# A two-layer decode kernel: queries and the first layer's gate and up with the weights as the moving operand

## The chip, the cores and the metric

The kernel runs on one core of a Trainium2 chip. The metric is device time in microseconds, the median of three runs. The profile is of one execution, and times inside it count from the start of its span.

## The reference

Two layers, each an attention block over a cache and a gated feed-forward block, for four sequences with one new token each:

```python
B, Sq, D = 4, 1, 512
Hq, Hkv, Sk, Dh = 32, 8, 8192, 128        # F = 1792, all bf16
def A(x, k_cache, v_cache, wq, wo):       # 4 query heads share one of the 8 cached heads
    q = (x @ wq) as (B, Hq, Sq, Dh)
    scores = einsum("bhqd,bhkd->bhqk", q, repeat(k_cache)) * Dh ** -0.5
    o = einsum("bhqk,bhkd->bhqd", softmax(scores), repeat(v_cache))
    return o as (B, Sq, Hq * Dh) @ wo
def B(x, w_gate, w_up, w_down):
    return (silu(x @ w_gate) * (x @ w_up)) @ w_down
x = x + A(layernorm(x)); x = x + B(layernorm(x))      # both twice, with the same weights
```

## The kernel before

The caches are 128 MB together and read in both layers; a few parts stay on the chip from one layer to the next. Everything else is small. So the program is written around one long stream of transfers, all issued by SyncE. Its order is the list `cmds`; `pump` issues the next entries as far as their place is free, and `freed(slot, a, b)`, called where an instruction that reads a place has been written, gives eighths (or halves of eighths) of a slot back. There are four slots of 4 MB and one more (`QS`), which first holds w_q, then K and V data.

The unit of attention work is a pair: two cached heads of one sequence, 16 pairs in a layer, K and V of a pair 4 MB each. For K, VectorE transposes blocks in place (`turn`, L558), TensorE computes scores with the queries as weights, laid out in `zq` with zeros around them (`scores`, L582), VectorE takes the maximum (`max_p`, `max_t`), ScalarE the exponential (`exps`, L629), VectorE transposes the result (`turn_p`, L646), and TensorE multiplies V (`values`, L718: four matmuls at a time, each in a quarter of the array's columns). The order of blocks is written out by hand with estimated due times (`drain`, `advance`, `line`). The output projection follows by groups of two heads and four sequences (`mix` L801, `rows` L836, `project` L861).

At the head of a layer, `center` subtracts the mean of x, and `qproj` multiplies by w_q: for every 128x128 block of w_q one matmul with that block as weights and four moving columns (L917, 128 of them a layer), then one scaling by `rstd` (L926), 16 small matmuls that bring the queries into the layout of the scores (L936), the placing of the first pair (`place_q`) and a copy for all others (L941). `deviation` (L903 to L907) computes `rstd`, with the logarithm of the scores' scale as a bias where queries are meant. In the second layer each eighth of w_q that has been read is freed for pieces of K.

At a layer's end `ffn` multiplies by gate and up with 128x128 weights and four moving columns (L961, 112 a layer), computes silu and the product (L975 to L982), and multiplies by w_down: in the first layer with w_down as weights (L999), in the second with hT as weights (L989). `WDS` lists which 128-row parts of w_down each transfer brings and how many rows stand side by side in a partition (the third number). The hidden index f must come in the same order out of gate and up; `base(L, fo)` says where the columns of part `fo` start and by how many elements they step, which is that third number.

Between the layers the slot that holds the first layer's weights is freed piece by piece by `ffn` and refilled with K of the second layer. A quarter of one K block stays in PSUM meanwhile (`hold`, L521 and L524); while it does (`held`), other small results go to bank 3.

Of the kernel before, what the change touches and what calls it, by code (L numbers as in the profile page):

```python
# [103 lines left out]
def bass_interleave_layers__gqa_block_cached__swiglu_ffn__decode_kernel(  # L104
# [40 lines left out]
    with ExitStack() as es:  # L145
# [14 lines left out]
        WDS = (((12, 14, 2), (10, 12, 2), (0, 2, 2), (2, 6, 4), (6, 10, 4)), ((0, 8, 2), (8, 12, 2), (12, 14, 2)))  # L160
# [26 lines left out]
        def base(L, fo):  # L187
            a, _, e = next(w for w in WDS[L] if w[0] <= fo < w[1])
            return a * P + (fo - a) // e * e * P + (fo - a) % e, e

        def wg_at(s, k, f, e):
            return columns(s * SL + k * F + f, e)

        def wu_at(s, k, f, e):
            o = k * F + f
            return columns((NSLOT + 1) * SL + o if o < RES else s * SL + O_WU + o - RES, e)
# [35 lines left out]
        head = sb("head", [P, H2], FP32)  # L232
        sel = sb("sel", [P, H2], FP32)
# [31 lines left out]
        qr = scr[:, 0:NQR].rearrange("p (c b g r) -> p c b g r", c=4, b=B, g=GP)  # L265
        made = scr[:, 0:2 * QB].bitcast(FP32)
        qT = scr[:, NQR:].rearrange("p (b h) -> p b h", b=B)
# [9 lines left out]
        def bank_bf(k):  # L277
# [6 lines left out]
        ROLE = {"step": (STEP, 0), "tot": (TOT, 128), "cmb": (LNB, 136), "out": (OUTB, 144), "mix": (LNB, 160), "ln": (LNB, 256),  # L284
                "q": (OUTB, 0)}
# [34 lines left out]
        for a in range(NA):  # L320
# [5 lines left out]
        T.op("dve", lambda e: e.memset(zq[:], 0.0), writes=["zq"])  # L326
# [15 lines left out]
             reads=["made"], writes=["own"])  # L342
        nc.scalar.preload_act_table_set("natural_log_exp_and_others")
# [3 lines left out]
        def pair_gb(u):  # L347
            return u // B, u % B

# [45 lines left out]
        cmds += [(K(1, us[2]), QS, a, b) for a, b in ((0, 1), (1, 2), (2, 4), (4, VIA))]  # L395
# [66 lines left out]
        def load_wd(w0, L, j, also=()):  # L462
            a, b, e_ = WDS[L][j]
            o = 0 if w0 is pTf else wd_from(L, a)
            T.dma("sp", w0[:, o:o + (b - a) * D].rearrange("p (m x) -> p m x", x=e_ * D),
                  B_w_down[a * P:b * P, :].rearrange("(m p e) n -> p m (e n)", p=P, e=e_), sem_w["wd"][j],
                  writes=[f"wd{j}"] + list(also))
# [95 lines left out]
        def place_q(L, u, eng="pool", q_of=qr, names=None):  # L563
            if (L, u) in placed_q:
                return
            placed_q.add((L, u))
            gp, b = pair_gb(u)
            shape = [P, 4, NA, REP]
            dst = zq[:, ZP:].rearrange("p (c a x) -> p c a x", c=4, a=NA)[:, :, :, 0:REP]
            q4 = q_of[:, :, b, gp, :].unsqueeze(2).to_broadcast(shape)  # L570
            m4_ = quad[:].unsqueeze(1).unsqueeze(3).to_broadcast(shape)
            T.op(eng, lambda e: e.tensor_tensor(dst, q4, m4_, ALU.mult),  # L572
                 reads=(names or ["qr"]) + ["quad"], writes=["zq"])

        def scores(L, u, q):
# [4 lines left out]
            for c in range(4):  # L580
                z0 = ZP + c * P - REP * q
                T.op("pe", lambda e: e.matmul(bank(bk)[:, 0:SW], lhsT=zq[:, z0:z0 + P], rhs=w[:, :, c // 2, :, c % 2],  # L582
                                              start=(q == 0 and c == 0), stop=(q == NB - 1 and c == 3)),
                     reads=names + ["zq"], writes=[f"pb{bk}"], sig=(c == 3))
# [29 lines left out]
        def exps(u):  # L614
            bk = SBK[turn_of[u]]
            i = turn_of[u]
            if summed:
# [4 lines left out]
            else:  # L622
# [4 lines left out]
            T.op("dve", lambda e: e.tensor_tensor_reduce(rsm, mine, head[:], 1.0, 0.0, ALU.mult, ALU.add, nm),  # L627
                 reads=[name, "head"], writes=["nm", "rsm"])
            T.op("act", lambda e: e.activation(pb[:], bank(bk)[:, 0:SW], ACTF.Exp, bias=nm, accum_out=rs),  # L629
                 reads=[f"pb{bk}", "nm"], writes=PB + ["rs"])  # L630
# [70 lines left out]
        def values(L, u):  # L701
# [71 lines left out]
            def combine():  # L773
# [5 lines left out]
                def scaled():  # L779
                    T.op("dve", lambda e: e.tensor_tensor(oT[:, gp * H2:(gp + 1) * H2, b], at, rl[:, turn_of[u], :], ALU.mult),  # L780
                         reads=[name, f"rl{turn_of[u]}"], writes=[OT[gp], "qT"])
# [10 lines left out]
        def mix(gs, fill):  # L792
# [4 lines left out]
            now = oT[:, gs[0] * H2:(gs[-1] + 1) * H2]  # L797
# [11 lines left out]
        groups = [[0, 1, 2, 3], [3, 0, 1, 2]]  # L809
        mixed, later = set(), []  # L810

        def close_group(L, gp, fill):
            if gp == groups[L][-1]:
                line.extend([[0.5, None, lambda: mix([gp], fill)], [0.7, None, lambda: out_proj(gp, fill)]])
                return
            if gp == 0:
                return
            gs = [0, 1] if gp == 1 else [gp]
            line.append([0.5, None, lambda: mix(gs, fill)])
# [13 lines left out]
        def rows(L, gp):  # L833
            for r in range(H2):
                h = gp * H2 + r
                T.op("pe", lambda e: e.matmul(bank(OUTB)[0:B, 0:D], lhsT=oT[:, h, :], rhs=wo_sb[:, h, :],  # L836
# [19 lines left out]
        def project(gp):  # L856
            at, name = place("out", 0, XB)
            for nt in range(KT):
                for r in range(H2):
                    h = gp * H2 + r  # L860
                    T.op("pe", lambda e: e.matmul(at[:, nt * B:(nt + 1) * B],  # L861
                                                  lhsT=wo_sb[:, h, pick2(nt)], rhs=oT[:, h, :],
# [3 lines left out]
        def out_proj(gp, fill):  # L866
            project(gp)
# [33 lines left out]
        def deviation(bias, bkey):  # L901
            at, name = (bank(SBK[1])[:, 0:B], f"pb{SBK[1]}") if held[0] else place("tot", 0, B)
            T.op("pe", lambda e: e.matmul(at, lhsT=ones, rhs=vs, start=True, stop=True),  # L903
                 reads=["vs", "onesf"], writes=[name])
            T.op("act", lambda e: e.activation(lnv, at, ACTF.Ln, scale=1.0 / D, bias=eps_sb[:]),
                 reads=[name, "eps"], writes=["lnv"])
            T.op("act", lambda e: e.activation(rstd[:], lnv, ACTF.Exp, scale=-0.5, bias=bias[:]),  # L907
                 reads=["lnv", bkey], writes=["rstd"])

        def qproj(L, u):  # L910
            at, name = place("ln", 0, Hq * B)
            for kt in range(KT):
                if kt == KT // 2:
                    deviation(lsc_sb, "lsc")
                for h in range(Hq):
                    q, last = 2 * kt + h * 2 // Hq, (h + 1) * 2 % Hq == 0
                    T.op("pe", lambda e: e.matmul(at[:, h * B:(h + 1) * B],  # L917
                                                  lhsT=wq_sb[:, kt, h * Dh:(h + 1) * Dh],
                                                  rhs=xn[:, kt * B:(kt + 1) * B],
                                                  start=(kt == 0 and h == 0), stop=(kt == KT - 1 and h == Hq - 1)),  # L920
                         reads=[WQ[q], "xn"], writes=[name], sig=last)
                    if L and last and q < NB - 2:
                        if q == NB - 3:
                            T._wait("act", T._need((), [WQ[q]]))
                        freed(QS, q, q + 1)
            T.op("dve", lambda e: e.tensor_tensor(qT, at.rearrange("p (h b) -> p b h", b=B),  # L926
                                                  rstd[:].unsqueeze(2).to_broadcast([P, B, Hq]), ALU.mult),
                 reads=[name, "rstd"], writes=["qT"] + OT)

            pick = ident.rearrange("p (c j e) -> p c j e", c=2, e=2)  # L930
            ob, oname = place("q", 0, NQR)
            ob = ob.rearrange("p (c b g r) -> p c b g r", c=4, b=B, g=GP)
            qv = qT.rearrange("p b (g h r) -> p b g h r", h=2, r=REP)
            for c in range(4):
                for a in range(NA):
                    T.op("pe", lambda e: e.matmul(ob[a * QB:(a + 1) * QB, c],  # L936
                                                  lhsT=pick[:, c // 2, :, c % 2],
                                                  rhs=qv[:, :, :, a // 2, :], start=True, stop=True),
                         reads=["qT", "ident"], writes=[oname], sig=(a == NA - 1))
            place_q(L, u, "dve", ob, [oname])  # L940
            T.op("dve", lambda e: e.tensor_copy(qr, ob), reads=[oname], writes=["qr", "made"])  # L941

        def ffn(L):
# [4 lines left out]
            fb = lambda ap: ap.rearrange("p (f b) -> p f b", b=B)  # L948
            rb = rstd[:].unsqueeze(1).to_broadcast([P, FO, B])
            rooms = {"wg0": room(s, 0, F), "wg1": room(s, F, 2 * F), "wg2": room(s, 2 * F, 3 * F), "wg3": room(s, 3 * F, O_WU), "wu0": [], "wu1": room(s, O_WU, O_WD)}  # L950
            for j, (a, b, _) in enumerate(WDS[L]):
# [3 lines left out]
            for at, wname, bk, ks in ((wg_at, "wg0", gb, (0, 1)), (wg_at, "wg1", gb, (1, 2)),  # L955
                                      (wg_at, "wg2", gb, (2, 3)), (wg_at, "wg3", gb, (3, KT)),
                                      (wu_at, "wu0", ub, (0, KT // 2)), (wu_at, "wu1", ub, (KT // 2, KT))):
                for fo in range(FO):
                    f = base(L, fo)
                    for kt in range(*ks):  # L960
                        T.op("pe", lambda e: e.matmul(bank(bk)[:, fo * B:(fo + 1) * B],  # L961
                                                      lhsT=at(s, kt, *f),
# [133 lines left out]
```

## Time and profile before

| | |
|---|---|
| median of three runs | 644.91 us (644.39 to 645.34) |
| the profiled execution | 645.21 us, of which the span 643.43 us |
| instructions | 7434, of which 3126 matmuls and 3128 weight loads |
| busy: PE, DVE, ACT, POOL | 65%, 66%, 7%, 2% of the span |
| DMA | 271.33 MB, the data queue's packets 99.0% of sixteen engines' span |
| mean granted clock of TensorE | 0.83 |

In lines of the profile, L and a number is a line of the kernel; "x" and a number counts instructions; PE is TensorE's matmuls, PEld its weight loads, DVE VectorE, ACT ScalarE, POOL GpSimd, SP SyncE. A timeline line has the start, the time, the engine, the line and the operation, and in brackets the idle time of the engine before it and what ended it. A line of the chain of waits has the start, the time and what the path ran through. The sixteen DMA engines share each transfer; a transfer counts as landed when all of them have finished their part.

### The profile page before, as it was taken

To read this page: it belongs to the slowest core of one execution; us is meant where nothing else is said; L and a number is where in the kernel's file an instruction comes from. 1 tells how busy PE (TensorE), PEld (TensorE's weight loads), DVE (VectorE), ACT (ScalarE), POOL (GpSimd) and SP (SyncE) were. 2 spreads that over 40 slices of the span, in tenths; PEclk is the share of its full clock that TensorE was granted. 3 is DMA by queue.
4 is the path that set the end of the run, shared out by engine and by line. 5 is a ranking of instruction groups with operands and counts; after the bars stand their busy time and mean duration, and the time that the engine had idled before them with its cause. 6 is when DMAs were issued, how large, how long until landed. Compare 5 with 4: busy or idle time off the path is not lost.

```text
span 643.4 us, 7434 instructions
## 1 busy us (share of the span) xinstructions
PE 416.7 (65%) x3126; PEld 180.0 (28%) x3128; DVE 421.7 (66%) x593; ACT 42.3 (7%) x118; POOL 11.6 (2%) x44
## 2 busy tenths in 40 slices
PE   0673376456765757757866977776555577557877
PEld 0421122112222322222226432332221232222324
DVE  5275467455776656776952688887765567755964
ACT  0000000000000000000010110000000000000110
POOL 0000000000000000000000000000000000000000
PEclk9995786698877889766975899999778887769877
DMA  9999999999999999999999999999999999999996
GB/s 372 442 424 416 430 444 426 431 424 429 438 436 423 428 433 439 426 426 431 440 406 380 416 431 431 436 429 425 432 435 432 427 430 438 429 428 429 440 408 257
DMA packets 15872, 271.79 MB, mean 422 GB/s; under 512 B 1624, under 2 KB 1632, under 8 KB 7264
## 3 DMA queue, kind: packets, MB, share of 16 engines
q1 hardware_dynamic: 15840, 271.33, 99.0%
q8 instruction: 24, 0.39, 0.2%
q14 instruction: 8, 0.07, 0.0%
HBM read 271.32 MB, written 0.00 MB: 422 GB/s over the span
## 4 chain that ended last, share of the span: by engine, by line
DMA 61%; DVE 19%; PE 15%; issue 3%; another core or an unknown queue 1%; SPq 0%; DVEq 0%
DMA kvf<-in_A_k_cache_dram 49%; DVE kvf L558 15%; DMA kvf<-in_A_v_cache_dram 11%; PE ps L582 9%; PE ps L718 2%; DVE pb L770 2%; DMA kvf<-in_B_w_down_dram 1%; PE ps L961 1%; PE ps L917 1%; DVE pb L766 0%; DVE pT L646 0%; DVE scr L780 0%; SPq L93 0%; PE ps L861 0%
## 5 line engine op out<-in xcount | busy, mean ns | idle before, releaser
L582 PE MATMUL ps<-kvf,zq 128*128 128x512 bf16 x1024 | 292.9, 432 | 183.5 <-DVE kvf L558 178.8
L558 DVE STREAM_TRANSPOSE kvf<-kvf 128x2048 f32<-128x2048 f32 (+1 forms) x133 | 280.5, 2132 | 128.4 <-DMA kvf<-in_A_k_cache_dram 128.0
L582 PEld LDWEIGHTS ps<-kvf,zq 128*128 128x128 bf16 x1024 | 99.1, 108 | 340.2 <-DVE kvf L558 222.6
L718 PE MATMUL ps<-kvf,pT 128*32 128x512 bf16 x960 | 67.6, 405 | 1.1 <-DVE pT L646 1.1
L629 ACT ACTIVATE pb<-ps,tiny 128x512 bf16<-128x512 f32 x32 | 22.0, 687 | 525.9 <-DVE tiny L627 505.1
L646 DVE STREAM_TRANSPOSE pT<-pb 64x512 bf16<-64x512 bf16 x60 | 41.2, 686 | 2.7 <-ACT pb L629 1.7
L770 DVE SCALAR_TENSOR_TENSOR pb<-ps,tiny,pb 128x128 f32<-128x128 f32 x104 | 36.5, 351 | 4.7 <-PE ps L718 0.8
L588 DVE TENSOR_REDUCE tiny<-ps 128x1 f32<-128x512 f32 x32 | 22.0, 687 | 20.1 <-PE ps L582 20.1
L718 PEld LDWEIGHTS ps<-kvf,pT 128*32 128x32 bf16 x960 | 21.0, 99 | 31.2 <-issue 16.0
L775 PEld LDWEIGHTS ps<-sel,pb 128*128 128x128 f32 x64 | 17.0, 273 | 16.5 <-DVE pb L770 8.3
L572 POOL TENSOR_TENSOR zq<-scr,tiny 128x64 bf16<-128x64 bf16 x30 | 9.0, 299 | 527.1 <-PE ps L582 527.1
L596 DVE TENSOR_REDUCE mrm<-ps 1x8 f32<-1x128 f32 x32 | 8.8, 275 | 13.6 <-PE ps L593 13.6
L775 PE MATMUL ps<-sel,pb 128*128 128x8 f32 x64 | 12.4, 267 | 5.8 <-DVE pb L770 5.8
L619 PEld LDWEIGHTS ps<-mrm,tiny 128*128 128x128 f32 x60 | 13.0, 223 | 9.2 <-DVE scr L780 3.2
L917 PE MATMUL ps<-xn,kvf 128*128 128x4 bf16 x256 | 7.5, 166 | 11.5 <-DMA kvf<-in_A_wq_dram 11.2
L766 DVE TENSOR_SCALAR pb<-ps,tiny 128x128 f32<-128x128 f32 x32 | 10.1, 315 | 3.0 <-PE ps L718 3.0
L619 PE MATMUL ps<-mrm,tiny 128*128 128x16 f32 x60 | 9.9, 241 | 3.1 <-ACT mrm L631 3.1
L836 PE MATMUL ps<-wo_sb,scr 128*4 128x512 bf16 x48 | 11.0, 379 | 0.5 <-DVE scr L805 0.5
L917 PEld LDWEIGHTS ps<-xn,kvf 128*128 128x128 bf16 x256 | 7.3, 105 | 11.8 <-DMA kvf<-in_A_wq_dram 11.4
L631 ACT ACTIVATE mrm<-head,tiny 128x8 f32<-128x8 f32 x32 | 9.6, 301 | 1.0
L593 PE MATMUL ps<-identf,tiny 128*1 128x128 f32 x32 | 8.7, 273 | 0.7 <-DVE tiny L588 0.7
L790 DVE TENSOR_TENSOR xT<-xT,ps 128x16 f32<-128x16 f32 x6 | 1.0, 171 | 10.4 <-PE ps L846 4.7
(87 smaller groups left out, 120.3 us busy)
## 6 DMA issues: line engine op xcount, KB each, us to landing
kvf<-in_A_k_cache_dram SPq DMA_DIRECT2D x27, 4096.0 KB, 31.2
kvf<-in_A_v_cache_dram SPq DMA_DIRECT2D x27, 4096.0 KB, 33.9
kvf<-in_A_v_cache_dram SPq DMA_DIRECT2D x3, 2048.0 KB, 25.2
kvf<-in_A_k_cache_dram SPq DMA_DIRECT2D x9, 512.0 KB, 7.9
kvf<-in_A_k_cache_dram SPq DMA_DIRECT2D x2, 2048.0 KB, 9.4
kvf<-in_A_wq_dram SPq DMA_DIRECT2D x2, 2048.0 KB, 18.1
wo_sb<-in_A_wo_dram SPq DMA_DIRECT2D x4, 1024.0 KB, 41.4
kvf<-in_B_w_gate_dram SPq DMA_DIRECT2D x2, 1792.0 KB, 23.9
```

The costliest lines, as they stand in the source:

```text
L558: T.op("dve", lambda e: e.transpose(w, w), reads=names, writes=names)
L582: T.op("pe", lambda e: e.matmul(bank(bk)[:, 0:SW], lhsT=zq[:, z0:z0 + P], rhs=w[:, :, c // 2, :, c % 2], start=(q == 0 and c == 0), stop=( ...
L588: T.op("dve", lambda e: e.tensor_reduce(mx[:], bank(bk)[:, 0:SW], AX.X, ALU.max), reads=[f"pb{bk}"], writes=["mx"])
L619: T.op("pe", lambda e: e.matmul(at, lhsT=ones, rhs=mrm[:, i * H2:(i + 2) * H2], start=True, stop=True), reads=[f"m8{i}", "rsm", "onesf"], ...
L629: T.op("act", lambda e: e.activation(pb[:], bank(bk)[:, 0:SW], ACTF.Exp, bias=nm, accum_out=rs), reads=[f"pb{bk}", "nm"], writes=PB + ["rs"])
L646: T.op("dve", lambda e: e.transpose(dst, pb[hp]), reads=["pb", "row"], writes=[name])
L718: T.op("pe", lambda e: e.matmul(bank(k)[j * QB:(j + 1) * QB, q0 * Dh:q1 * Dh], lhsT=p_t[:, t, h, :], rhs=v[:, q0:q1, t, :], start=((last o ...
L766: T.op("dve", lambda e: e.tensor_scalar(into, o, own[:, q:q + 1], None, op0=ALU.mult), reads=[f"pb{k}", "own"], writes=["row"] if last els ...
L770: T.op("dve", lambda e: e.scalar_tensor_tensor(into, o, own[:, q:q + 1], into, op0=ALU.mult, op1=ALU.add), reads=[f"pb{k}", "own", iname], ...
L775: T.op("pe", lambda e: e.matmul(at, lhsT=into, rhs=sel[:], start=True, stop=True), reads=[iname, "sel"], writes=[name])
L836: T.op("pe", lambda e: e.matmul(bank(OUTB)[0:B, 0:D], lhsT=oT[:, h, :], rhs=wo_sb[:, h, :], start=(gp == groups[L][0] and r == 0), stop=(g ...
L917: T.op("pe", lambda e: e.matmul(at[:, h * B:(h + 1) * B], lhsT=wq_sb[:, kt, h * Dh:(h + 1) * Dh], rhs=xn[:, kt * B:(kt + 1) * B], start=(k ...
```

## The change

Queries. `qproj` now takes the normalised x as weights (128 rows, four columns) and 512 columns of w_q as the moving operand, in each of the four quarters of the array's columns, so that one pass over a row block of w_q is two times four matmuls instead of 32. w_q's two halves of heads go to two PSUM banks. In the second layer the half that holds the first pair's heads comes first, and the freed eighths go out in that order. VectorE transposes each bank (`on_end`), four small copies place the first pair, and eight copies on ScalarE (`spread`) give the layout from which `place_q` takes the others. The queries are no longer scaled: `rstd` enters as the scale of the exponential, and `headr` (the mask of heads times `rstd`) in its bias.

First layer's gate and up. The same exchange: 448 columns of the weights move through each quarter, one matmul for each (one strip is cut in two where its data lie in two places), and VectorE transposes the two results.

w_down. Its rows are dealt differently, in both layers. In the first, partition p holds rows 14p to 14p+13. In the second, the rows side by side in a partition become 8, 4 and 2 for the three transfers (2 before), and the gate and up columns follow.

Also: output groups of the second layer are kept in the order of their use (`spot`), and its first three groups are mixed together; a VectorE memset of two PSUM banks comes at the start.

The diff, cut:

```diff
-        WDS = (((12, 14, 2), (10, 12, 2), (0, 2, 2), (2, 6, 4), (6, 10, 4)), ((0, 8, 2), (8, 12, 2), (12, 14, 2)))
+        WDS = (((12, 14), (10, 12), (0, 2), (2, 6), (6, 10)), ((0, 8), (8, 12), (12, 14)))
+        WDE = (8, 4, 2)
...
-        def base(L, fo):
-            a, _, e = next(w for w in WDS[L] if w[0] <= fo < w[1])
+        def base(fo):
+            j = next(j for j, w in enumerate(WDS[1]) if w[0] <= fo < w[1])
+            a, e = WDS[1][j][0], WDE[j]
             return a * P + (fo - a) // e * e * P + (fo - a) % e, e
...
+        T.op("dve", lambda e: e.memset(ps[:, SBK[1] * BANKF:(OBK[0] + 1) * BANKF], 0.0),
+             writes=[f"pb{SBK[1]}", f"pb{OBK[0]}"])
...
-        cmds += [(K(1, us[2]), QS, a, b) for a, b in ((0, 1), (1, 2), (2, 4), (4, VIA))]
+        cmds += [(K(1, us[2]), QS, a, b) for a, b in ((1, 2), (3, 4), (0, 1), (2, 3), (4, VIA))]
...
-            T.dma("sp", w0[:, o:o + (b - a) * D].rearrange("p (m x) -> p m x", x=e_ * D),
-                  B_w_down[a * P:b * P, :].rearrange("(m p e) n -> p m (e n)", p=P, e=e_), sem_w["wd"][j],
-                  writes=[f"wd{j}"] + list(also))
+            dst, src = w0[:, o:o + (b - a) * D], B_w_down.rearrange("(p f) n -> p (f n)", f=FO)[:, a * D:b * D]
+            if L:
+                dst = dst.rearrange("p (m x) -> p m x", x=WDE[j] * D)
+                src = B_w_down[a * P:b * P, :].rearrange("(m p e) n -> p m (e n)", p=P, e=WDE[j])
+            T.dma("sp", dst, src, sem_w["wd"][j], writes=[f"wd{j}"] + list(also))
...
-            T.op("dve", lambda e: e.tensor_tensor_reduce(rsm, mine, head[:], 1.0, 0.0, ALU.mult, ALU.add, nm),
-                 reads=[name, "head"], writes=["nm", "rsm"])
-            T.op("act", lambda e: e.activation(pb[:], bank(bk)[:, 0:SW], ACTF.Exp, bias=nm, accum_out=rs),
+            T.op("dve", lambda e: e.tensor_tensor_reduce(rsm, mine, headr[:, b, :], 1.0, 0.0, ALU.mult, ALU.add, nm),
+                 reads=[name, "headr"], writes=["nm", "rsm"])
+            T.op("act", lambda e: e.activation(pb[:], bank(bk)[:, 0:SW], ACTF.Exp, bias=nm, scale=rstd[:, b:b + 1],
+                                                  accum_out=rs),
...
-            gs = [0, 1] if gp == 1 else [gp]
+            gs = groups[L][:n + 1] if n == (1, 2)[L] else [gp]
...
+            def on_end(k):
+                src = bank(QK[k]).rearrange("p (x i e) -> p x e i", i=QB, e=2)
+                dst = bank(TO[k]).rearrange("p (i x e) -> p x e i", i=QB, e=2)
+                T.op("dve", lambda e: e.transpose(dst, src), reads=[f"pb{QK[k]}"], writes=[f"pb{TO[k]}"])
...
+            for n in range(NB):
+                k, kt = (first, 1 - first)[n // KT] if L else n % 2, n % KT if L else n // 2
+                q = 2 * kt + k
+                if n == NB // 2:
+                    scales = deviation(lsc_sb, "lsc", SBK[0], False)
+                    if L:
+                        on_end(first)
+                        place_first()
+                        scales()
+                for a in range(NA):
+                    f = ((2 * k + a % 2) * 2 + a // 2) * W2
+                    T.op("pe", lambda e: e.matmul(bank(QK[k])[a * QB:a * QB + B, :],
+                                                  lhsT=xn[:, kt * B:(kt + 1) * B], rhs=wq_sb[:, kt, f:f + W2],
+                                                  start=(kt == 0), stop=(kt == KT - 1)),
+                         reads=[WQ[q], "xn"], writes=[f"pb{QK[k]}"], sig=(a == NA - 1))
...
+                blk = bank(k)[:, 0:FW].rearrange("p (i f) -> p f i", f=FO)
+                T.op("dve", lambda e: e.transpose(blk, blk), reads=[f"pb{k}"], writes=[f"pb{k}"])
...
+                for kt in range(*ks):
+                    parts = [(0, *base(fo), fo) for fo in range(FO)] if L else [(a, f, w, 0) for a, f, w in strips(bk == ub, kt)]
+                    for n, (a, f, w, fo) in enumerate(parts):
+                        x = xn[:, kt * B:(kt + 1) * B]
+                        if L:
+                            to, lhs, rhs = bank(bk)[:, fo * B:(fo + 1) * B], at(s, kt, f, P, w), x
+                        else:
+                            to, lhs, rhs = bank(bk)[a * QB:a * QB + B, f - a * FW:f - a * FW + w], x, at(s, kt, f, w)
...
+                on_end(1 - pair_gb(us[0])[0] // 2)
+            spread()
```

## The prediction

> **What bounds the kernel now.** I read the page first: how full the DMA engines are.
>
> ```profile
> DMA  9999999999999999999999999999999999999996
> ...
> q1 hardware_dynamic: 15840, 271.33, 99.0%
> q8 instruction: 24, 0.39, 0.2%
> ```
>
> The sixteen DMA engines are busy in every slice but the last: from 3 us on, the kernel is one stream of 271 MB. What an engine saves counts only where the stream runs dry or after it ends. So next the chain of waits over the end, from the landing of the last values on.
>
> ```profile
> 585.97 43.37 DMA kvf<-in_A_v_cache_dram
> ...
> 635.46 0.84 PE ps L961 x28
> 636.29 0.22 PE ps L903 x2
> 636.52 2.22 PE ps L961 x84
> 638.74 0.52 PE ps L879 x8
> 639.26 1.49 PE ps L989 x47
> 640.75 0.03 issue
> 640.78 0.42 PE ps L989 x8
> ```
>
> The values land at 629.3; behind them stand 14 us in which nearly nothing overlaps, and 3.1 us of these are the second layer's 112 gate and up matmuls (L961) on PE. Then the boundary between the layers, by the timeline, and the same line at the end:
>
> ```profile
> 343.94 1.85 PE L961 MATMUL ps<-xn,kvf 128*128 128x4 bf16 x56
> ...
> 346.24 1.00 PE L961 MATMUL ps<-xn,kvf 128*128 128x4 bf16 x28 [0.45 <-DMA kvf<-in_B_w_up_dram]
> ```
> ```profile
> 636.38 2.36 PE L961 MATMUL ps<-xn,kvf 128*128 128x4 bf16 x84
> ...
> 639.17 1.99 PE L989 MATMUL ps<-kvf,pb 128*4 128x128 bf16 x56
> ```
>
> At the boundary PE itself waits for transfers (and again 0.90 us for w_down at 349.25); at the end its matmuls are the path. The last view is the end by stretches of 1 us (length; busy us of PE, PE's loads, DVE, ACT, POOL; clock, DMA share, GB/s):
>
> ```profile
> 638.00:639.00 1.00, 1.00 (x36) 0.96 (x33) 0.83 (x4) 0.00 (x0) 0.00 (x0) 0.50 0.32 123
> 639.00:640.00 1.00, 1.00 (x38) 0.74 (x32) 0.11 (x1) 0.00 (x0) 0.00 (x0) 0.50 0.13 49
> ```
>
> PE's clock is 0.50 here, and the DMA share (0.32, 0.13, from 1.02 at 634 to 636) falls in steps: the engines finish one by one. Each transfer is spread over sixteen and is complete with the slowest. The completion records of the last w_down transfer run from 635.98 to 640.73; those of the first K spread over 0.44 us. The slowest engine's lag over the fastest grew in steps of 1.2 to 1.4 us (0.38 to 1.59, 1.7 to 3.1, 2.1 to 3.39, 3.6 to 4.92), each beside a 16 KB packet of the instruction queue (1.0 to 1.1 us on one engine; 24 on the page). The slowest engine sets every landing.
>
> **Part by part: the w_q product.** Each layer's 128 matmuls that load 128x128 weights and the 16 that pick (L936) become 32 with 512 moving columns, four at a time in the array's quarters. The values matmuls (L718) have that form: four start within 10 ns, a round takes 216 ns at full clock and 427 ns at half. At the boundary (clock 0.50) eight rounds are 3.4 us, and the 128 loads at 26.7 ns were 3.4 us too: PE gains nothing there. What goes is the way to the first scores. After half the rounds (1.7 us) DVE transposes 512 columns (0.6 us, half of L521's 1.22 us for 1024) and four small copies of 0.2 to 0.3 us on two engines place the first pair, beside the second half. Scores start when that half ends, near 356.7 instead of 357.7. The other DVE transpose (0.6), headr (0.3) and eight ACT copies (2 us) come after the two transposes of L521, where qT, the placing and the copy (0.29, 0.23, 0.41 us) went ahead of them; the second pair needs them at 366. If that cover were gone, 3 us would show. This microsecond is worth nothing: the slots that those scores free are refilled by a queue that is not empty. The thinnest point is 343.6: what is issued then starts on the slowest engine at 347.3, more than 2 us after it could. In the first layer the first scores come about 0.7 us later (both transposes ahead of them), before a wait of 8 us for the next K (33.7). The scale in the exponential makes one operand of ACT (L629, 0.69 us) a column: nothing, or at most 0.1 us under the stream.
>
> **Pieces.** The order of K pieces into w_q's place changes, and one piece of 1 MB with 8 KB rows is now two with 4 KB rows. By the packet records (314 ns for 8 KB, 165 ns for 4 KB) that is 128x314/16 = 2.51 us against 256x165/16 = 2.64: **+0.13 us** on the stream.
>
> **First layer's gate and up.** 112 matmuls become 33 of up to 448 columns (0.37 us a round): gate 1.5 us against 1.7, the last half of up 0.8 against 1.0. Two transposes of 448 columns (0.55 us each) are added; the gate's lies under the 0.45 us wait for w_up and what slack the silu has, up's is on the path. hT comes 0.3 us later, and the next w_down group waits 0.9 us for its landing anyway: **0**. Without that cover 0.3 us of PE, not of the stream.
>
> **Second layer's w_down.** Not in the change's few words, but in its diff: the rows per partition go from 2, 2, 2 to 8, 4, 2, so packets of 2 KB (86 ns) become 8 and 4 KB. 1 MB and 0.5 MB take 2.51 and 1.32 us instead of 2.76 and 1.38, together 0.31 us, of which at most 0.2 us of wait is there to be had (L989 pauses twice).
>
> Its price: gate and up columns must follow the same order, and `base` now steps by 8 elements for 64 of those 112 weight loads, by 4 for 32, by 2 for 16; all 112 stepped by 2. Line L961 prices two steps. At the end 84 with step 2 take (2.36 - 0.17)/83 = 26.4 ns each. In the first layer, at the same clock, 32 of the 56 step by 4: (1.85 - 0.17)/55 = 30.6 on average, so (56x30.6 - 24x26.4)/32 = 33.8 ns: **+7 ns**. Step 8 (16 bytes) is not in this form in the trace; the nearest row is the load of 32 columns with that step, L801, beside L718's with none:
>
> ```profile
> L801 PEld LDWEIGHTS ps<-scr,identf x96: 134/156/165, 209.8 to 632.7; 128*32 128x32 bf16 x96
> ...
> L718 PEld LDWEIGHTS ps<-kvf,pT x960: 92/97/151, 45.4 to 625.5; 128*32 128x32 bf16 x192
> ```
>
> Median 156 against 97 ns (L936, 8 bytes apart: 126), and L801's rounds of four follow each other every 59 ns at either clock, with only 8 columns to move. I treat one load of 128 columns (26.7 ns when contiguous, L917) like four such loads side by side, an estimate, and take 59 ns: +32.3. Bounds: 26.4 (no cost), and 67 (step 4 spends 33.8 ns on 64 runs of two elements, step 8 has twice as many runs). Sum: 64x32.3 + 32x7 = **2.3 us** more PE on the path that ends last. Nothing covers it: up's end releases hT (L982), then L989; silu's 1.5 us run beside up and are longer covered. The two waits of L989 vanish in it (-0.2): **+2.1 us**; ends -0.2 and +2.6. The strided gr, gw, hT operands cost nothing: L596 reads with that step, 128 elements in 0.28 us.
>
> The Trainium skill (SBUF — State Buffer, Specifications (TRN2)) speaks against this part: lines are of 16 bytes, and full bandwidth needs at least two hits in each. By it step 4 would be free and step 8 pay; the trace agrees on the direction but already charges 7 ns for two hits.
>
> **Instruction packets.** 303 matmuls with their loads go (2x112 + 79), 606 of PE's 6254 instructions; 0.39 MB over 6254 is 63 bytes, so 38 KB or 2.3 of the 16 KB packets. About 4 of the 22 before the values' landing hit the slowest engine; 4/22 x 2.3 x 1.25 us = **-0.5 us**, an estimate. Which engine a packet hits isn't to be foreseen: bounds -1.2 and +1.2 us.
>
> **Others.** Eight output rows matmuls of the first group in the second layer move to 585 (24 in place of 16, 1.8 us more): PE is idle 4.6 us behind them.
>
> **Sum.** The profiled execution took 645.21 us (span 643.43 and 1.8 around it), 0.30 over the median 644.91. 645.21 + 2.1 + 0.13 - 0.5 = 646.9, so a median of **646.6**.
>
> **Rivals.** *The step is free.* Then the second layer's FFN costs as before, or 0.64 - 0.2 us if 8 is charged like 4. For it: step 4 cost only 7 ns; against it: L801. The Trainium skill (TensorE: Matmul & The Clock Gate, Weight-path perf modes) keeps the fast load for any column step up to 1,024 elements. 644.91 + 0.4 + 0.13 - 0.5 = 645.0, not slower; 0.20. *The step is free and the slowest engine loses a whole packet or two:* 644.91 - 0.2 + 0.13 - 1.2 = 643.6, or less; 0.10. *Quarters don't overlap:* the four strips run one after another, gate takes 16x0.37 = 6 us instead of 1.7, and what its passes free is issued up to 4 us later. It decides from the 2 us that the slowest engine has in hand: 646.6 + 2 to 4 = 649 to 651. Against it L718's starts; 0.06. Forecast: 0.62, within it 0.14 that the packets bring it under +0.2%. The rest, 0.02, anything else, slower.
>
> **Numbers.** A measurement tells about 0.2% (1.3 us) from none. The free step's 0.20 fall to 0.17 same, 0.02 slower, 0.01 faster. Slower: 0.48 of the forecast, 0.06, 0.02 and 0.02: 0.58. Same: 0.14 + 0.17 = 0.31. Faster: 0.10 + 0.01 = 0.11. The range runs from the free step with half a packet more gained (645.0 less 0.8) to the 67 ns load (+0.5), no packet gain (+0.5) and half a packet's loss (+0.6): 644.2 to 648.2.
>
> **What would show it.** L961 at the end: 84 matmuls in about 4 us instead of 2.36, at step 8 one in 59 ns; L989 without pauses; the chain unchanged up to there; the DMA row full across the boundary; w_q's line near 3.4 us plus the deviation; 21 or 22 packets on q8; the last values landing within 1.2 us of 629.3. Wrong if step 8 runs at 27 to 34 ns, if the DMA row shows a hole near 345 to 360, or if the values land more than 1.3 us away.

## The result, and the profile after

The changed kernel takes **647.31 us** (median of 6 runs, 646.29 to 647.91), the kernel before 644.86 (6 runs, 644.39 to 645.36): ratio **1.0035**, 95% interval 1.0022 to 1.0048. It is slower by 2.45 us; the forecast was 646.6 and slower. The profiled execution after took 647.37 us, with a span of 645.1 (before: 645.21 and 643.43).

The stream first, on the page after, as read before:

```profile
DMA  9999999999999999999999999999999999999995
...
q1 hardware_dynamic: 15472, 271.33, 98.8%
q8 instruction: 22, 0.36, 0.2%
```

It is as full as it was up to the last slice, across the boundary too; the 271.33 MB are the same, and two instruction packets fewer were fetched (22 for 24). Next, the chain of waits over the end, from the issue of the last values:

```profile
585.66 43.05 DMA kvf<-in_A_v_cache_dram
...
634.95 1.44 PE ps L1041 x28
636.38 0.43 PE ps L931 x2
636.81 4.03 PE ps L1041 x84
640.85 0.52 PE ps L907 x8
641.37 1.58 PE ps L1069 x42
```

The steps are the same as before, under new line numbers (L1041 was L961, L931 was L903, L907 was L879, L1069 was L989). The transfer of values on this chain lands at 628.72, 0.6 us earlier than before; the second layer's 112 gate and up matmuls then take 1.44 + 4.03 us where they took 0.84 + 2.22. The same stretch by the timeline of PE (start, length, line, matmuls; idle time ahead in brackets):

```profile
634.88 1.50 PE L1041 MATMUL ps<-xn,kvf 128*128 128x4 bf16 x28
...
636.67 4.17 PE L1041 MATMUL ps<-xn,kvf 128*128 128x4 bf16 x84
640.77 0.59 PE L907 MATMUL ps<-identf,xT 128*4 128x64 f32 x8
641.22 1.67 PE L1069 MATMUL ps<-kvf,pb 128*4 128x128 bf16 x56
```

1.50 - 0.84 and 4.17 - 2.36 make +2.47 us of PE on the path; L1069 has lost its two pauses (1.67 for 1.99). The 84 are 48 loads at step 8, 24 at step 4 and 12 at step 2: with 0.17 us off for the last matmul's own length, and 32 and 26 ns for steps 4 and 2 (priced below), (4.00 - 24 x 0.032 - 12 x 0.026)/47 = 62 ns for one at step 8.

The windows of 1 us (busy us of PE, PE's loads, DVE, ACT, POOL; clock, DMA share, GB/s) tell whether the transfers or PE held this stretch:

```profile
638.00:639.00 1.00, 1.00 (x25) 1.00 (x23) 0.73 (x3) 0.26 (x1) 0.00 (x0) 0.50 0.28 111
639.00:640.00 1.00, 1.00 (x25) 1.00 (x24) 0.72 (x2) 0.00 (x0) 0.00 (x0) 0.50 0.11 43
640.00:641.00 1.00, 1.00 (x26) 0.98 (x26) 0.12 (x1) 0.00 (x0) 0.00 (x0) 0.50 0.08 23
```

PE is full and starts 25 matmuls in a microsecond. The kernel before, on the same line and at the same granted clock of 0.50, started 44:

```profile
637.00:638.00 1.00, 1.00 (x44) 1.00 (x41) 0.62 (x3) 0.40 (x2) 0.00 (x0) 0.50 0.63 229
```

The load port was full then too, so what has changed is the time of one load. The transfers run out beside it.

The boundary between the layers, by the timeline of PE:

```profile
344.21 1.66 PE L1041 MATMUL ps<-kvf,xn 128*4 128x448 bf16 x16
346.34 0.91 PE L1041 MATMUL ps<-kvf,xn 128*4 128x448 bf16 x9 [0.47 <-DMA kvf<-in_B_w_up_dram]
...
349.49 0.59 PE L1079 MATMUL ps<-pb,kvf 128*128 128x4 bf16 x16 [0.35 <-DMA kvf<-in_B_w_down_dram]
...
352.72 1.88 PE L996 MATMUL ps<-kvf,xn 128*4 128x512 bf16 x16 [0.27 <-DVE xn L919]
354.53 0.59 PE L931 MATMUL ps<-pb,tiny 128*128 128x4 f32 x2
355.05 1.88 PE L996 MATMUL ps<-kvf,xn 128*4 128x512 bf16 x16
356.86 1.37 PE L607 MATMUL ps<-kvf,zq 128*128 128x512 bf16 x3
```

The same two places before:

```profile
349.25 0.58 PE L999 MATMUL ps<-pb,kvf 128*128 128x4 bf16 x16 [0.90 <-DMA kvf<-in_B_w_down_dram]
...
357.71 0.61 PE L582 MATMUL ps<-kvf,zq 128*128 128x512 bf16 x1 [0.35 <-DVE zq L572]
```

The quarters overlap (16 matmuls of 512 columns in 1.88 us are 0.47 us for each four), the first scores start at 356.86, 0.85 us earlier than before, and the wait for w_down has shrunk from 0.90 to 0.35 us: most of what up's transpose adds came out of that wait.

### The profile page after: what moved, and what is told of

It reads as the page before. It is cut to its first block, busy times and chain, and to the rows that moved or that the text cites. A ratio compares the mean times of both kernels' runs of the same rounds, so it can differ in the third digit from the quotient of the medians.

```text
span 645.1 us, 6824 instructions
## 1 busy us (share of the span) xinstructions
PE 414.8 (64%) x2807; PEld 172.3 (27%) x2809; DVE 426.3 (66%) x599; ACT 50.2 (8%) x138; POOL 11.9 (2%) x44
## 3 DMA queue, kind: packets, MB, share of 16 engines
q1 hardware_dynamic: 15472, 271.33, 98.8%
## 4 chain that ended last, share of the span: by engine, by line
DMA 60%; DVE 20%; PE 15%; issue 4%; ACT 0%; SPq 0%; POOL 0%; ACTq 0%; DVEq 0%; POOLq 0%
DMA kvf<-in_A_k_cache_dram 45%; DVE kvf L581 15%; DMA kvf<-in_A_v_cache_dram 11%; PE ps L607 8%; DMA kvf<-in_A_wq_dram 3%; PE ps L745 2%; DVE pb L797 2%; PE ps L1041 1%; DMA kvf<-in_B_w_down_dram 1%; PE ps L996 1%; DVE pT L673 1%; DVE pb L793 1%; DVE ps L547 0%; DVE scr L807 0%; PE ps L889 0%
## 5 line engine op out<-in xcount | busy, mean ns | idle before, releaser
L745 PE MATMUL ps<-kvf,pT 128*32 128x512 bf16 x960 | 65.8, 396 | 1.5 <-DVE pT L673 1.5
L655 ACT ACTIVATE pb<-ps,tiny 128x512 bf16<-128x512 f32 x32 | 24.9, 777 | 507.7 <-DVE tiny L653 489.2
L996 PE MATMUL ps<-kvf,xn 128*4 128x512 bf16 x64 | 7.5, 621 | 11.1 <-DMA kvf<-in_A_wq_dram 10.8
L807 DVE TENSOR_TENSOR scr<-ps,rl 128x8 bf16<-128x8 f32 x32 | 5.7, 177 | 3.2 <-PE ps L802 2.2
L745 PE MATMUL ps<-kvf 128*32 128x512 bf16 (+2 forms) x96 | 5.5, 361 | 3.4 <-DMA kvf<-in_A_v_cache_dram 3.3
## 6 DMA issues: line engine op xcount, KB each, us to landing
kvf<-in_A_v_cache_dram SPq DMA_DIRECT2D x3, 2048.0 KB, 26.4
```

Source lines behind the costliest of these rows:

```text
L745: T.op("pe", lambda e: e.matmul(bank(k)[j * QB:(j + 1) * QB, q0 * Dh:q1 * Dh], lhsT=p_t[:, t, h, :], rhs=v[:, q0:q1, t, :], start=((last o ...
L996: T.op("pe", lambda e: e.matmul(bank(QK[k])[a * QB:a * QB + B, :], lhsT=xn[:, kt * B:(kt + 1) * B], rhs=wq_sb[:, kt, f:f + W2], start=(kt ...
```

## The experiments

**The second layer's w_down dealing taken back.** The kernel after, with 2, 2, 2 rows per partition again.

```
-        WDE = (8, 4, 2)
+        WDE = (2, 2, 2)
```

> The changed kernel with the second layer's w_down dealt 2, 2, 2 rows to a partition again, so that all its gate and up loads step by 2 elements; the queries and the first layer's gate and up stay as changed. Theory (the step of the weight loads is the whole loss): the 84 matmuls at the end go from 4.17 us back to 2.36, the first 28 from 1.50 to 0.84, and the time falls by 2.2 us (2.47 less the 0.2 us that L989's pauses come back with) to about 645.0, the time of the kernel before within 0.1%. Rival (the moving-weights products and their transposes cost at the boundary, or the program's own start and end, which took 0.5 us more around the span): the time stays at 646.5 or above, with the stretch from the values' landing to the end as short as before.

Measured: 645.20 us (median of 11 runs) beside 645.17 for the kernel before, ratio 0.9996 (0.9985 to 1.0007). Its timeline of PE at the end:

```profile
635.61 0.85 PE L1041 MATMUL ps<-xn,kvf 128*128 128x4 bf16 x28
636.32 0.57 PE L931 MATMUL ps<-pb,tiny 128*128 128x4 f32 x2
636.75 2.38 PE L1041 MATMUL ps<-xn,kvf 128*128 128x4 bf16 x84
```

The line has its old times, and the kernel its old time. The w_q product in quarters, the scale in the exponential, the split pieces, the first layer's gate and up and the fewer instruction packets make together no difference that 11 runs can tell.

**The dealing alone.** The kernel before, with the rows per partition of the kernel after.

```
-        WDS = (((12, 14, 2), (10, 12, 2), (0, 2, 2), (2, 6, 4), (6, 10, 4)), ((0, 8, 2), (8, 12, 2), (12, 14, 2)))
+        WDS = (((12, 14, 2), (10, 12, 2), (0, 2, 2), (2, 6, 4), (6, 10, 4)), ((0, 8, 8), (8, 12, 4), (12, 14, 2)))
```

> The kernel before with only the dealing of the second layer's w_down changed to 8, 4, 2. Theory: all of the loss without the rest of the change: 84 matmuls in about 4.2 us, L989 without pauses, 644.9 + 2.47 - 0.2 = 647.1. Rival (the loss is elsewhere): 644.6 to 644.9, since the packets of w_down are larger and nothing else differs.

Measured: 646.98 us (9 runs) beside 645.17, ratio 1.0029 (1.0019 to 1.0039). The timeline of PE:

```profile
635.00 1.51 PE L961 MATMUL ps<-xn,kvf 128*128 128x4 bf16 x28
636.37 0.57 PE L903 MATMUL ps<-pb,tiny 128*128 128x4 f32 x2
636.80 4.18 PE L961 MATMUL ps<-xn,kvf 128*128 128x4 bf16 x84
640.91 0.59 PE L879 MATMUL ps<-identf,xT 128*4 128x64 f32 x8
641.28 1.71 PE L989 MATMUL ps<-kvf,pb 128*4 128x128 bf16 x56
```

One line of the diff, put into the kernel before, gives the same two groups (1.51 and 4.18) and 1.8 us. With the run above this settles the main cause from both sides. The wider packets bring nothing: L989 has lost its pauses, since it now starts (641.28) later than w_down lands (640.04).

**The price by the column step.** The kernel before, with 24 extra matmuls at each of six steps in an idle stretch of PE in the first layer (their results go to a bank that nobody reads then). The part for step 8:

```
+            for _ in range(24):
+                one(8, lambda e: e.matmul(at, lhsT=w[:, 0:8*127+1:8], rhs=x, **args))
```

> The kernel before with 144 more small matmuls in the first layer's third pair, far from the end: 24 each with 128x128 weights whose columns step by 1, 2, 4, 8, 16 and 32 elements, four moving columns. Prediction's line: 26 ns each at steps 1 and 2, 33 at 4, 59 at 8 (between 53 and 67). What the changed kernel's end shows, (4.17 us for 48 of step 8, 24 of 4, 12 of 2), asks for about 63 at step 8. Theory of 16-byte lines: no dearer beyond 8, since each element has a line of its own already. Rival (a cost that grows with the distance): steps 16 and 32 dearer again.

The starts of the matmuls in the trace follow each other every 25, 25, 33, 60, 61 to 62 and 62 ns at steps 1, 2, 4, 8, 16 and 32. The groups of instructions (busy us and mean ns of one after the bar; lines 704, 706, 708, 710, 712 and 714 are steps 1, 2, 4, 8, 16 and 32):

```profile
L712 PEld LDWEIGHTS ps<-xn,wo_sb 128*128 128x128 bf16 x24 | 1.6, 162 | 0.0
L714 PEld LDWEIGHTS ps<-xn,wo_sb 128*128 128x128 bf16 x24 | 1.6, 169 | 0.0
L710 PEld LDWEIGHTS ps<-xn,wo_sb 128*128 128x128 bf16 x24 | 1.5, 161 | 0.0
...
L708 PEld LDWEIGHTS ps<-xn,wo_sb 128*128 128x128 bf16 x24 | 0.9, 117 | 0.0
...
L706 PEld LDWEIGHTS ps<-xn,wo_sb 128*128 128x128 bf16 x24 | 0.7, 97 | 0.0
L704 PEld LDWEIGHTS ps<-xn,wo_sb 128*128 128x128 bf16 x24 | 0.7, 96 | 0.4 <-issue 0.4
```

The load itself lengthens, from 96 to 161 ns, and the price stops rising at step 8, where the two-byte weights stand 16 bytes apart: a wider step costs no more. Step 2 is free. The granted clock fell meanwhile (1.00 in 92 to 94 us, 0.82 in 94 to 96, 0.50 in 96 to 98), but it doesn't make the price: at 0.50 a load at step 2 took 26.4 ns at the end of the kernel before, and one at step 8 62 ns in the kernel after. The whole kernel took 645.25 us in its one run.

**Step 4 in place of 8.** The kernel after once more, with 4, 4, 2.

```
-        WDE = (8, 4, 2)
+        WDE = (4, 4, 2)
```

> The kernel after, with w_down's rows per partition 4, 4, 2 in the second layer instead of 8, 4, 2: 96 of the 112 gate and up loads step by 4 elements, 16 by 2. If the price is one of the column step as measured in the kernel after (31 to 33 ns at step 4, 26 at step 2), the 84 matmuls at the end take 84 x 32 less 16 x 6 = about 2.6 us and the 28 before them 0.9 us, and the time is 0.5 to 0.7 us over the same kernel at 2, 2, 2 (645.2): 645.6 to 646.0. If the loss hung on the dealing as such and not on the step of the loads (the wider packets landing worse, say), it stays near 647.

Measured: 645.40 us (11 runs) beside 645.13, ratio 1.0008 (0.9999 to 1.0017). The timeline of PE:

```profile
634.11 1.06 PE L1041 MATMUL ps<-xn,kvf 128*128 128x4 bf16 x28
635.03 0.57 PE L931 MATMUL ps<-pb,tiny 128*128 128x4 f32 x2
635.46 2.85 PE L1041 MATMUL ps<-xn,kvf 128*128 128x4 bf16 x84
```

1.06 + 2.85 is 0.68 us over the 0.85 + 2.38 at step 2, as the price by step says (a little above the 2.6 and 0.9 expected). In the medians only 0.2 of it shows (645.40 for 645.20, each with its own runs of before), which these intervals can't part from 0.68; the time is slightly under the range expected, and far from 647. Rows that are twice as wide do no harm that these runs can tell.

**The second layer's gate and up moving too.** The kernel after, with the quarters form in both layers, and 14 rows of w_down per partition; no strided loads are left.

```
-            if L:
-                dst = dst.rearrange("p (m x) -> p m x", x=WDE[j] * D)
-                src = B_w_down[a * P:b * P, :].rearrange("(m p e) n -> p m (e n)", p=P, e=WDE[j])
...
-            fb = lambda ap: ap.rearrange("p (f b) -> p b f" if L else "p (b f) -> p b f", b=B)
+            fb = lambda ap: ap.rearrange("p (b f) -> p b f", b=B)
...
-                if L:
-                    return
                 blk = bank(k)[:, 0:FW].rearrange("p (i f) -> p f i", f=FO)
...
-                    parts = [(0, *base(fo), fo) for fo in range(FO)] if L else [(a, f, w, 0) for a, f, w in strips(bk == ub, kt)]
+                    parts = [(a, f, w, 0) for a, f, w in strips(bk == ub, kt)]
...
```

> The changed kernel with the second layer's gate and up also moving in four quarters, and w_down dealt 14 rows to a partition in both layers (8, 4, 2 KB packets, no strided load). Theory (the loss is the strided weight loads and nothing else): gate and up are 33 matmuls, 1.5 us of rounds if the clock is still full at 635 and 3.0 if it is half, one transpose of 0.67 us on the path, and then w_down's landing near 640.5 ends it: 644.4 to 645.6. Rival (quarters and transposes cost as much as they save): 646.5 or more.

Measured: 645.86 us (11 runs), ratio 1.0016 (1.0007 to 1.0025) to before, and 0.3 us above the range expected. The timeline of PE:

```profile
635.29 0.55 PE L1033 MATMUL ps<-kvf,xn 128*4 128x448 bf16 x8
635.77 0.59 PE L928 MATMUL ps<-pb,tiny 128*128 128x4 f32 x2
636.29 2.41 PE L1033 MATMUL ps<-kvf,xn 128*4 128x448 bf16 x25
638.49 0.64 PE L904 MATMUL ps<-identf,xT 128*4 128x64 f32 x8
640.41 0.95 PE L1061 MATMUL ps<-kvf,pb 128*4 128x128 bf16 x56 [1.28 <-DVE pb L1054]
```

PE is through with gate and up at 638.7, but then waits 1.28 us for DVE, which has two transposes (0.67 and 0.66 us) more on the way to hT; w_down's last transfer, which had been expected to end it, lands at 640.41, when PE starts on w_down. This beats the kernel after and not the kernel before: the path moved from PE to DVE. None of the versions run beats the kernel before.

**Instruction packets.** The prediction took 0.5 us off for 2.3 fewer packets. To make such a term large enough to be seen, the kernel before got small matmuls more in PE's waits of the first layer: 80 behind each of eight pairs, and in a second kernel 160.

```
+            for _ in range(80):
+                one(1, lambda e: e.matmul(at, lhsT=w[:, 0:P], rhs=x, **args))
...
+                    if L == 0 and 2 <= u <= 9:
+                        small_matmuls()
```

> The kernel before, with 640 small matmuls more (128x128 contiguous weights, 4 columns, into a bank that nobody reads) in the first layer, 80 behind each of eight pairs, where PE otherwise waits 9 us for the next K: 1,280 PE instructions of 63 bytes, 81 KB, 4.9 more packets of 16 KB on the instruction queue (29 instead of 24). If each such packet holds up one of the sixteen DMA engines and about one in five or six of them falls on the engine that ends last (4 of 22 before the values' landing at 1.25 us each, 0.23 us a packet), the values land later and the kernel takes 1.1 us more, with bounds of 0 and 3 us, since which engine a packet hits isn't to be foreseen. If instruction packets cost nothing: the same time within 0.3 us.

> The same with 160 small matmuls behind each of the eight pairs, 1,280 in all: 161 KB, 9.8 more packets (34). PE's own 4.3 us a pair still lie in its wait of 9 us. If each packet costs 0.23 us by way of the slowest DMA engine: 2.2 us more than before, some 647.4, and the lag of the slowest engine over the fastest at the last values grows from 4.9 us by about 2. If packets cost nothing: the same time within 0.3 us. If PE's work rather than its code were what costs, the stream would show PE or its clock in the chain of waits ahead of K's landings.

Measured: with 640 more 645.34 us (11 runs; before 645.13), ratio 1.0001 (0.9993 to 1.0010); with 1,280 more 646.48 (8 runs), ratio 1.0027 (1.0017 to 1.0037). The row of the page for the instruction queue (packets, MB, share), with 640 and then with 1,280:

```profile
q8 instruction: 29, 0.48, 0.3%
```
```profile
q8 instruction: 34, 0.56, 0.3%
```

The packets came as reckoned (5 and 10 more). The first dose costs nothing that these runs can tell: by the interval -0.5 to +0.6 us, so the 0.23 us a packet from which 1.1 us was expected is ruled out. The second costs 1.35 us in the medians and 1.1 to 2.4 by the interval, which leaves the 2.2 expected just inside. A smaller steady price, 0.11 to 0.13 us a packet, would fit both. What the packets did in the profiled executions stands in the completion records. They are compared here with the profiled execution of before: first and last of the sixteen engines, and their mean, for the transfers that land at these times in the kernel before (us, + is later):

```
last landing,     640 matmuls more          1,280 matmuls more
before            first   mean   last       first   mean   last
160.6             -0.07  +0.14  -0.01       -0.03  +0.47  +1.64
277.5             -0.01  +0.43  +1.27       -0.08  +0.94  +2.78
346.1             -0.13  +0.32  -0.18       -0.08  +0.93  +1.42
351.7             +0.55  +0.83  +1.46       +1.01  +1.45  +1.57
373.8             +0.61  +0.42  -0.33       +2.45  +2.01  -0.02
386.1             +1.26  +0.74  -0.35       +2.69  +2.43  +1.69
570.9             +1.34  +0.74  +0.93       +2.73  +2.44  +2.39
591.6             +1.35  +0.75  -0.34       +2.94  +2.44  +2.05
635.0             +1.37  +0.77  -0.29       +2.93  +2.44  +2.11
```

Within the first layer the mean moves by 0.09 us a packet (0.43 for 5, 0.94 for 10 at 277.5); times sixteen that is 1.4 to 1.5 us of one engine, an estimate, while the first engine stays where it was: the stream absorbs it. At the boundary (346 to 386) it is settled. There PE waits for w_up and w_down, so for the last engine, and each issue that follows a freed slot comes later. With 1,280 the last engine was 1.42 us late at 346.1, the issues from 362 on came 2.7 us late, and the early engines ran dry (first +2.45; the DMA share of 340 to 350 was 0.93, against 0.99 before). With 640 the last engine was on time at 346.1 (-0.18), because in between the kernel before's own last engine had fallen back by about as much (its lag grew from 2.0 to 3.1 us). But the transfer of 351.7 had its last engine 1.46 us late, the issues from 362 on came 1.4 us late here too, and the first engine was 1.3 us late from 386 on. That this execution ends no later owes something to which engines were hit: at 570.9 its last engine was still 0.93 us late, and then the lag in the kernel before grew from 3.6 to 4.9 us, while here it stayed at 3.2. So the records show how a packet can cost, by way of the last engine at the boundary and the issues behind it; they don't show that five always cost nothing and ten always something. With 1,280 the lag at the end is 4.1 us; it had been expected to grow from 4.9 by about 2. PE's own work was not in the way: its timeline still shows an idle time of 4.40 us ahead of the next K after a round of 160. That it is the added code and not another effect of the added matmuls rests on these records; a kernel with the code and without the work was not tried.

## Why the prediction was right, point by point

- **The w_q product** (0): as forecast. At the boundary the scores start 0.85 us earlier (1 forecast), in the first layer 1.1 us later (26.96 for 25.86; 0.7 forecast), and neither shows in the time (the first experiment). The transposes of 512 columns took 0.73 and 0.69 us at the boundary, not 0.6; the first lies beside the second half of the product. The exponential rose from 687 to 777 ns with its scale, at the upper end of 0 to 0.1, under the stream.
- **Pieces** (+0.13): too small to be told apart here.
- **First layer's gate and up** (0): hT is ready 0.74 us later (348.01 for 347.27), not 0.3. Up's second half ends where it ended before (346.34 + 0.91 for 346.24 + 1.00; 0.2 us less was forecast), and its transpose of 0.67 us, not 0.55, comes on top. The cover held, though with little left: the wait for w_down fell from 0.90 to 0.35 us. In the profiled executions with 2, 2, 2 and with both layers moving, that wait was gone (24 matmuls run on without a pause from 349.11 and 348.98), and only the next one, for the last w_down group (0.64 and 0.56 us), was left; no cost shows in the time with 2, 2, 2.
- **Second layer's w_down** (+2.1, with ends -0.2 and +2.6): this is the change. A load at step 8 measured 60 to 62 ns (59 taken, from L801's rounds of four), at step 4 32 to 33 (33.8). More PE on the path: 2.47 us (2.3). In whole times, the dealing alone cost 1.8 us in the kernel before, with an interval of 1.2 to 2.5. The Trainium skill (SBUF — State Buffer, Specifications (TRN2)), which asks for at least two hits in each 16-byte line for full bandwidth, has the direction right, and the end of the rise at step 8, one weight a line, agrees with it; but at step 4, with two hits, a load already took 33 ns for 25. The rival in which the step is free has fallen: 60 ns for 25. With it goes the reading that the Trainium skill's fast load for any step up to 1,024 (TensorE: Matmul & The Clock Gate, Weight-path perf modes) would make step 8 free.
- **Strided operands** (0): L1062, on the path, took 0.28 us where L982 took 0.21, so 0.07 us were missed.
- **Instruction packets** (-0.5): this step failed. The landing was 0.6 us earlier in the profiled execution, which looks like agreement, but the experiments take that away. The landing of the values' very last transfer in the profiled executions with 21 to 25 packets runs from 629.01 to 630.61, with no order by packets (22 packets: 629.01, 629.97, 630.01; 24: 630.07, 630.61). The kernel with two packets fewer and the old dealing takes as long as before; its interval (-1.0 to +0.5 us) alone would still leave room for -0.5, but the 640 extra matmuls rule out the 0.23 us a packet that the term was made of. The step took the share of packets that hit the slowest engine as an average price. In the records a packet counts only by way of the engine that somebody waits for; how much that is on average, the two doses don't settle.
- **The sum**: 0.7 us short (646.6 for 647.31), though the measured difference is known only to 1.4 to 3.1 us, and the forecast's 1.7 lies in it. Without the packet term, which no run bears out, the forecast would have been 647.1. In the span the profiled executions gained +1.7 (645.1 for 643.4), as forecast, but partly by the luck of an early landing; in the medians of the spans it is +1.9 (645.1 for 643.2). The rest lies outside the span. The time around it was 2.27 us in the median of the kernel after (1.95 to 2.41), and 1.78 in the profiled execution before (1.74 to 2.07 in the 49 runs of before beside the experiments). Values above 2.07 occur in three kernels alone: the kernel after (4 of 6 runs), with 2, 2, 2 (4 of 11) and with 4, 4, 2 (3 of 11). The kernel before with step 8 stays at 1.76 to 1.83, so the dealing doesn't make it; something in the new instructions may, in some executions, though with both layers moving it never exceeded 1.88. Of the profiled executions the one of the kernel after alone is long there, and it alone has an 8 KB instruction packet at 647.26, 2.1 us behind the end of the span, so a fetch at the program's end may be the reason; that was not tried and stays open. With the terms as now measured: 644.86 + 1.9 (1.0029) + 0.4 is 647.2.

## What to carry to other kernels

A new deal of rows over partitions that makes a transfer's packets wider can turn up as a column step in somebody's weight loads: look for who must follow the order, and price those loads, not the transfer. Where the stream has ended and PE is the path, as here, 64 loads at 60 instead of 25 ns (2.2 us) outweigh the 0.2 us of waiting that the wider packets could have saved. And before a difference of half a microsecond in one profiled execution is given to a cause, look how far that landing wanders among executions in which the cause is the same.

## What the runs showed of the hardware

A load of 128x128 bf16 weights with 4 moving columns costs 25 ns at column steps 1 and 2, 33 at 4 and 60 to 62 at 8, 16 and 32: the rise has an end. An instruction packet of 16 KB set one DMA engine back by an estimated 1.4 to 1.5 us (the mean of the sixteen by 0.09 us a packet), more than its own 1.0 to 1.1 us. Ten more of them were worth 1.35 us and five nothing that 11 runs could tell. In the records a lag of one engine is free until somebody waits for that engine and issues stop behind it.
